# A fused retention and mixer kernel: the order of the front, VectorE's share of the query copies, and the places of two weight loads

## The chip, the cores and the metric

The kernel runs on one core of a Trainium2 chip. The metric is device time in microseconds (us). In this document TensorE, VectorE, ScalarE, GpSimd and SyncE go by the names of the profile: PE (with PEld for its weight loads), DVE, ACT, POOL and SP. SP issues the hardware DMA queue (q1 in the profile). POOL issues the software DMA queue (q0), the one that turns float32 into bf16 on its way. A tile is a buffer in on-chip memory; PSUM is the memory that PE writes and that DVE and ACT read back.

## The reference

Inputs are q, k and v of 8 batches, 8 heads, 576 positions and 64 values, in float32, and the weights of a mixer.

```python
scores = scale * np.matmul(q, k.transpose(0, 1, 3, 2))
Dmat = np.where(rel >= 0, gamma[:, None, None] ** rel[None, :, :], 0.0)
x = np.matmul(scores * Dmat, v)            # then heads side by side: (8, 576, 512)
h = x.transpose(0, 2, 1) @ U @ V           # mixing over positions, rank 32
u = x + h.transpose(0, 2, 1)
out = u + np.maximum(u @ w_ch1, 0.0) @ w_ch2   # 512 -> 2048 -> 512
```

Since the decay is a product of powers of gamma, the kernel runs attention as a recurrence over blocks of positions. It scales v by gamma to the minus position, keeps a running sum of k times v (the state), adds the masked part inside a block, and scales the result by gamma to the position.

## The kernel before

Batches go in pairs, and each pair has nine chunks of 128 positions. The first pair is treated apart, since all else waits for it. Its 1152 positions are four **units** of 256 positions (0 and 1 in batch 0, 2 and 3 in batch 1) and one chunk J, whose lower half (LO) ends batch 0 and whose upper half (HI) begins batch 1.

A unit takes these steps, with the lines of the code:

- Six loads on the SP queue, two halves each of k, q and v (`load_u`, L595), 256 KB each. Below "the second half of unit two's q" is the fourth of unit 2's six loads.
- POOL casts k and q to bf16 (`cast_u`, L613), and POOL (once DVE) scales v (`scale_u`, L617).
- PE turns k and q (`T_u`, 8 transposes at L628 each); DVE or ACT copies the turned tile out of PSUM (L639, L641). Keys (j = 1) are copied straight, queries (j = 0) are written with a step of two elements.
- PE multiplies for the scores (`SC_u`, L656), DVE masks them (`mask_u`, L664), PE multiplies by v (`RV_u`, L685), adds to the state (`ST_u`, L713; ACT copies the state in `Sblk`, L722), adds queries times state (`QS_u`, L694), and DVE writes x (`XS_u`, L702).

The half chunk J has the same steps in small (`T_J` L739, `SC_J` L752, `mask_J` L761, `RV_J` L771, `QS_J` L779, `XS_J` L786). `startup` runs units 0 and 1 and J's lower half. It then turns x (`to_xT`, L891), runs the first step of mixing (`MA`, L427: 20 matmuls into a PSUM tile that ACT casts to `a_sb`, L433), adds `a_sb` times V onto the turned x (L913), and copies the sum to `uT` (L922 on ACT, L924 on DVE). `warm` (L189) issues matmuls whose result nobody reads; they keep PE busy where it would wait.

`first_stretch` then mixes three things on PE in the order in which the code writes them: blocks of **Y1**, the first product of the channel mixer (16 blocks f0 to f15 for batch 0, four matmuls of 128x512 each, L513, each followed by a ReLU on ACT, L518), J's upper half, and units 2 and 3. Calls `y(n)` set the Y1 blocks between the others. Y1 needs the weights w1, which POOL loads in four quarters (`load_w1`, L195, 512 KB of bf16 each): quarter 0 for f0 to f3, quarter 1 for f4 to f7, and so on. POOL issues them in its program order, between its casts.

Nothing is rescheduled by a planner: the program order written here is the order on each engine, and each instruction waits for the data, the buffers and the DMAs that it needs. From about 50 us on the kernel is a steady alternation: Y1 and Y2 (L547) on PE, with attention of the following batch and DMA transposes spread between them by `merge`.

Of the kernel before, what the change touches and what calls it, by code (L numbers as in the profile page):

```python
# [9 lines left out]
FP32 = mybir.dt.float32  # L10
# [26 lines left out]
def kernel(  # L37
# [11 lines left out]
    nc = tc.nc  # L49
# [144 lines left out]
    def load_w1(fb):  # L194
        nc.gpsimd.dma_start(  # L195
            out=w1_sb[:, :, fb * W1B:(fb + 1) * W1B],
            in_=moe_w_ch1[:, fb * W1B:(fb + 1) * W1B].rearrange("(c p) f -> p c f", p=P),
        )
# [214 lines left out]
    def mixer_items(pr, par, split=False):  # L413
# [5 lines left out]

        def MA(where=None):
            pool_, tag = where or (ps_s, "pss")
            pa = pool_.tile([P, P], FP32, tag=tag, name="pa")
            for n, i in enumerate(idx):
                for cc in range(NCC):
                    nc.tensor.matmul(  # L427
                        pa[cc * R:(cc + 1) * R, :], Ub[:, n, :],
                        st["x", pr][:, i, cc * P:(cc + 1) * P],
                        start=(n == 0), stop=True, skip_group_check=True,  # L430
                    )
            a_sb = a_pool.tile([P, P], BF16, tag="a_sb", name="a_sb")
            nc.scalar.activation(out=a_sb, in_=pa, func=AF.Copy)  # L433
            st["a", par] = a_sb
            if par == 0:
                st["u", 0] = u_pool.tile([P, 4, dm], BF16, tag="u0", name="u0")
                st["uT", 0] = uT_pool.tile([P, 4, NCC, P], BF16, tag="uT0", name="uT0")
            else:
                st["u", 1] = u_pool.tile([P, 5, dm], BF16, tag="u1", name="u1")
                st["uT", 1] = uT_pool.tile([P, 5, NCC, P], BF16, tag="uT1", name="uT1")  # L440
# [54 lines left out]
        items.append(lambda: None)  # L495
        return items

    def y1_items(par, by_seg=False):
        nch = 4 + par
        segs = [(0, 4)] if par == 0 else [(0, 3), (3, 2)]  # L500
        if by_seg:
            segs = [(1, 4), (0, 1)]
        items, made = [], []

        def Y1(f, seg):
            if not made:
                made.append(1)
                st["y1", par] = y1_pool.tile(
                    [P, NF, nch * P], BF16, tag=f"y1{par}", name="y1")
            c0, n = segs[seg]  # L510
            ps = ps_big.tile([P, 4, P], FP32, tag="big", name="ps_y1")
            for cc in range(NCC):
                nc.tensor.matmul(  # L513
                    ps[:, 0:n, :], w1_sb[:, cc, f * P:(f + 1) * P],
                    st["uT", par][:, c0:c0 + n, cc, :],
                    start=(cc == 0), stop=(cc == NCC - 1),
                )
            nc.scalar.activation(  # L518
                out=st["y1", par][:, f, c0 * P:(c0 + n) * P],
                in_=ps[:, 0:n, :].rearrange("p s t -> p (s t)"), func=AF.Relu)  # L520

        ns = len(segs)
        for f in range(NF):
            items.append((nch * 216.0, lambda f=f: [Y1(f, g) for g in range(ns)]))
        if by_seg:
            return Y1, items
        return items
# [96 lines left out]
    def T_u(u, j, eng):  # L624
        pst = ps_big.tile([P, 2 * NHP, P], BF16, tag="big", name="pst")
        for jj in range(2):
            for hp in range(NHP):
                nc.tensor.transpose(  # L628
                    pst[:, jj * NHP + hp, :], un[u][j][:, jj, hp * P:(hp + 1) * P], ident)
        t = qkT_pool.tile([P, 2 * NHP, P], BF16, tag="qkT", name="qkT")  # L630
        un[u]["T", j] = t
        o, i_ = t, pst
        if j == 0:

            o = t.rearrange("p a b -> p (a b)").rearrange(
                "p (hp t j) -> p j hp t", hp=NHP, j=2)
            i_ = pst.rearrange("p (j hp) t -> p j hp t", j=2)
        if eng is nc.scalar:
            nc.scalar.activation(out=o, in_=i_, func=AF.Copy)  # L639
        else:  # L640
            eng.tensor_copy(out=o, in_=i_)  # L641

    def qT(u):
        return un[u]["T", 0].rearrange("p a b -> p (a b)").rearrange(
# [167 lines left out]
    def startup():  # L812
# [14 lines left out]
        T_u(0, 1, nc.vector)  # L827
        warm(5)
        nc.scalar.activation(out=V_b, in_=V_f, func=AF.Copy)
        T_u(0, 0, nc.scalar)  # L830
        make_v()
        warm(3)
        SC_u(0, 0, ps_sc, "psc")
# [3 lines left out]
        SC_u(0, 1, ps_o, "po")  # L837
        mask_u(0, 1)
        warm(2)
        T_u(1, 0, nc.scalar)  # L840
        scale_u(0, 0, nc.gpsimd)
        load_w1(0)
        scale_u(1, 0, nc.gpsimd)
        scale_u(1, 1, nc.gpsimd)
        cast_qk(0, J, LO, nc.gpsimd, js=(0,))
        scale_v(0, J, LO, nc.gpsimd)
        load_w1(1)
        cast_qk(0, J, HI, nc.gpsimd)
        scale_v(0, J, HI, nc.gpsimd)
        load_w1(2)  # L850
# [20 lines left out]
        warm(1, ps_big, "big")  # L871
        ST_u(1, LO, accB, False)
        Sblk(accB, 2)
        warm(1, ps_big, "big")
        RV_u(1, 0)
        RV_u(1, 1)
        T_J(LO, nc.vector)
        ST_u(1, HI, accB, False)
        Sblk(accB, 3)
        SC_J(LO)  # L880
        mask_J(LO)
        QS_u(1, 0, 1)
        QS_u(1, 1, 2)
        XS_u(1)
# [14 lines left out]
        RV_J(LO)  # L899
        QS_J(3)  # L900
        XS_J(LO)
        warm(2, ps_sc, "psc")
        xT.append(ps_sc.tile([P, dm], FP32, tag="psc", name="xT"))
        for i in range(2, J):
            to_xT(i, range(3))
        for i in range(J):
            to_xT(i, (3,))
        MA, _, _, _ = mixer_items(0, 0, split=True)
        MA((ps_o, "po"))
        warm(1)  # L910
        for cc in range(NCC):
            g = slice(cc * R, (cc + 1) * R)
            nc.tensor.matmul(  # L913
# [17 lines left out]

    def first_stretch():

        ys = iter([fn for _, fn in y1_items(0)])

        def y(n):
            for _ in range(n):
# [3 lines left out]

        _, MH0, _, outs0 = mixer_items(0, 0, split=True)
        MA1, MH1, MT1, outs1 = mixer_items(0, 1, split=True)
        y(1)
        make_uo()
        y(3)
        T_J(HI, nc.scalar, ps_s, "pss")
        y(1)
        SC_J(HI)
# [4 lines left out]
        Sblk(acc, 0)  # L954

        def unit(u, slots, last):
            if last:
                load_w1(u)
            for hh in range(2):
                cast_u(u, 1, hh, nc.gpsimd)  # L960
            cast_u(u, 0, 0, nc.gpsimd)
            cast_u(u, 0, 1, nc.gpsimd)
            if last:
                load(*order[NI], (1, 0, 2), gate=True)
                load(*order[NI + 1], (1, 0, 2))
            scale_u(u, 0, nc.gpsimd)
            scale_u(u, 1, nc.gpsimd)
            if not last:
                y(1)
            T_u(u, 1, nc.vector)  # L970
            T_u(u, 0, nc.scalar)
            y(2)
            SC_u(u, 0, ps_sc, "psc")
            mask_u(u, 0)
            y(1)
            ST_u(u, LO, acc, False)
            Sblk(acc, slots[1])
            SC_u(u, 1, ps_sc, "psc")
            mask_u(u, 1)
            if not last:  # L980
                RV_u(u, 0)
                ST_u(u, HI, acc, False)
                Sblk(acc, slots[2])
            else:
                y(1)
                load(*order[NI + 2], (1, 0, 2))
                RV_u(u, 0)
            QS_u(u, 0, slots[0])
            QS_u(u, 1, slots[1])
            RV_u(u, 1)  # L990
            XS_u(u)
            if last:
                RV_J(HI)
                XS_J(HI)
# [132 lines left out]
```

## Time and profile before

| what | us |
|---|---|
| three runs, median (lowest, highest) | 320.07 (319.88, 322.36) |
| the profiled execution, its own time | 320.66 |
| its span, first to last instruction | 318.7 |
| PE busy | 311.4 |
| DVE, ACT, POOL busy | 169.1, 136.7, 90.3 |
| PE's named waits after 50 us | 0.2 |

The span is what the trace's clock covers; 1.96 us of the execution's own time lie outside it. "Busy" adds up the durations of an engine's instructions. The profile models the ends of matmuls, so a busy PE is not necessarily at its peak. A wait is the idle time of an engine before an instruction, put down to whatever came last. The mean granted clock of PE was 1.000.

### The profile page before, as it was taken

To read this page: it belongs to the slowest core of one execution; us is meant where nothing else is said; L and a number is where in the kernel's file an instruction comes from. 1 tells how busy PE (TensorE), PEld (TensorE's weight loads), DVE (VectorE), ACT (ScalarE), POOL (GpSimd) and SP (SyncE) were. 2 spreads that over 40 slices of the span, in tenths; PEclk is the share of its full clock that TensorE was granted. 3 is DMA by queue.
4 is the path that set the end of the run, shared out by engine and by line. 5 is a ranking of instruction groups with operands and counts; after the bars stand their busy time and mean duration, and the time that the engine had idled before them with its cause. 6 is when DMAs were issued, how large, how long until landed. Compare 5 with 4: busy or idle time off the path is not lost.

```text
span 318.7 us, 9166 instructions
## 1 busy us (share of the span) xinstructions
PE 311.4 (98%) x3929; PEld 167.7 (53%) x3929; DVE 169.1 (53%) x354; ACT 136.7 (43%) x293; POOL 90.3 (28%) x138
## 2 busy tenths in 40 slices
PE   8999899999999999999999999999999999999996
PEld 3564554554444444466644444466644444467544
DVE  5571466447995467545684468545674563500012
ACT  2757557772120465038720375048720463057400
POOL 5762933512232423132241423141241300110000
DMA  7999999999999979699994999598994710620022
GB/s 202 258 204 267 232 198 203 191 203 187 237 212 216 260 156 175 137 242 183 176 184 106 262 177 175 142 248 172 163 202 109 189 37 1 135 81 0 2 84 81
DMA packets 151321, 53.30 MB, mean 167 GB/s; under 512 B 131985, under 2 KB 148753, under 8 KB 151281
## 3 DMA queue, kind: packets, MB, share of 16 engines
q1 hardware_dynamic: 144512, 40.40, 70.2%
q0 software_dynamic: 6768, 12.32, 16.2%
q8 instruction: 30, 0.49, 0.7%
q14 instruction: 11, 0.08, 0.1%
HBM read 36.85 MB, written 9.44 MB: 145 GB/s over the span
## 4 chain that ended last, share of the span: by engine, by line
PE 84%; DMA 7%; ACT 3%; DVE 2%; issue 1%; SPq 1%; POOL 1%; ACTq 0%
PE ps_y L513 37%; PE ps_y L547 35%; DMA stage_t<-in_q_dram 5%; DMA qkT<-qk 2%; PE psc L279 2%; PE ph L454 1%; PE po L344 1%; PE ps_y L558 1%; PE po L361 1%; SPq L595 1%; PE psc L290 1%; PE pa L427 1%; ACT qkT L639 1%; PE psc L656 1%; PE pst L628 1%
## 5 line engine op out<-in xcount | busy, mean ns | idle before, releaser
L518 ACT ACTIVATE y<-ps_y 128x384 bf16<-128x384 f32 (+2 forms) x192 | 89.1, 489 | 105.1 <-PE ps_y L513 104.6
L513 PE MATMUL ps_y<-uT,w_sb 128*128 128x512 bf16 (+3 forms) x768 | 132.2, 326 | 0.7 <-ACT uT L922 0.4
L547 PE MATMUL ps_y<-w_sb,y 128*128 128x512 bf16 x560 | 126.3, 379 | 0.0
L513 PEld LDWEIGHTS <-w_sb 128*128 128x128 bf16 x768 | 70.2, 98 | 51.0 <-issue 2.4
L547 PEld LDWEIGHTS <-y 128*128 128x128 bf16 x560 | 52.7, 98 | 61.3
L536 DVE TENSOR_TENSOR o_sb<-ps_y,u 128x512 f32<-128x512 f32 (+2 forms) x38 | 25.2, 663 | 66.3 <-PE ps_y L547 63.9
L303 DVE TENSOR_TENSOR ret<-psc,tri 64x256 bf16<-64x256 f32 x108 | 45.3, 419 | 1.1
L539 POOL DMA_DIRECT2D out_dram<-o_sb x31 | 17.3, 558 | 98.6 <-DVE o_sb L536 95.7
L255 POOL TENSOR_TENSOR vt<-stage_t,vscale 128x512 bf16<-128x512 f32 (+1 forms) x29 | 30.2, 1041 | 52.3 <-DMA stage_t<-in_v_dram 44.6
L325 DVE TENSOR_TENSOR s_f<-psc,s_f 128x256 f32<-128x256 f32 x42 | 17.8, 423 | 26.2 <-PE psc L290 12.9
L460 DVE TENSOR_TENSOR u<-ph,xt 128x1024 bf16<-128x1024 f32 (+3 forms) x24 | 21.8, 951 | 9.3 <-PE ph L454 9.3
L246 ACT ACTIVATE qk<-stage_t 128x512 bf16<-128x512 f32 x27 | 16.9, 626 | 21.1 <-DMA stage_t<-in_q_dram 15.2
L372 DVE TENSOR_TENSOR xt<-po,qscale 128x512 bf16<-128x512 f32 x27 | 18.4, 681 | 1.8 <-PE po L344 1.8
L244 POOL CAST qk<-stage_t 128x512 bf16<-128x512 f32 x20 | 12.3, 614 | 23.6 <-DMA stage_t<-in_k_dram 21.4
L334 ACT ACTIVATE s_sb<-s_f 128x512 bf16<-128x512 f32 (+1 forms) x27 | 15.5, 575 | 3.8 <-DVE s_f L325 3.8
L315 DVE COPY vs<-vt 64x256 bf16<-64x256 bf16 x54 | 14.3, 265 | 1.2
L664 DVE TENSOR_TENSOR ret<-psc,triU 128x1024 bf16<-128x1024 f32 x8 | 9.6, 1222 | 9.2 <-PE psc L656 9.2
L189 PE MATMUL pw<-ident 128*128 128x512 bf16 x34 | 11.5, 461 | 1.4 <-POOL ident masks.py:199 1.4
L613 POOL CAST qk<-stage_t 128x512 bf16<-128x512 f32 x16 | 9.6, 613 | 9.9 <-DMA stage_t<-in_q_dram 5.3
L323 DVE COPY s_f<-psc 128x256 f32<-128x256 f32 x6 | 2.5, 424 | 16.4 <-PE psc L290 11.3
L279 PEld LDWEIGHTS <-qkT 64*64 64x64 bf16 x432 | 5.6, 107 | 9.6 <-issue 8.5
L433 ACT ACTIVATE a_sb<-pa 128x128 bf16<-128x128 f32 x8 | 2.2, 277 | 18.0 <-PE pa L427 18.0
(112 smaller groups left out, 191.4 us busy)
## 6 DMA issues: line engine op xcount, KB each, us to landing
stage_t<-in_k_dram SPq DMA_DIRECT2D x32, 256.0 KB, 4.8
stage_t<-in_q_dram SPq DMA_DIRECT2D x32, 256.0 KB, 5.3
stage_t<-in_v_dram SPq DMA_DIRECT2D x32, 256.0 KB, 5.5
out_dram<-o_sb POOLq DMA_DIRECT2D x31, 256.0 KB, 4.3
w_sb<-in_moe_w_ch_dram POOLq DMA_DIRECT2D x4, 512.0 KB, 8.0
w_sb<-in_moe_w_ch_dram POOLq DMA_DIRECT2D x8, 256.0 KB, 5.8
stage_t<-in_k_dram SPq DMA_DIRECT2D x8, 128.0 KB, 5.1
stage_t<-in_q_dram SPq DMA_DIRECT2D x8, 128.0 KB, 5.5
```

What stands on the lines that cost most here:

```text
L246: nc.scalar.activation(out=t[rows, 0, :], in_=c["f", 0][rows].rearrange("p h d -> p (h d)"), func=AF.Copy)
L255: (eng or nc.gpsimd).tensor_tensor(out=c["v"][rows], in0=c["f", 2][rows], in1=vscale[rows, i, :, None].to_broadcast([n, H, D]), op=ALU.mult,)
L303: nc.vector.tensor_tensor(out=ret[o, n], in0=c["psc"][t, hl, 0:SW].rearrange("p (hp i) -> p hp i", i=D), in1=tri[t, None, t].to_broadcast( ...
L325: nc.vector.tensor_tensor(out=f[:, t, :], in0=inc, in1=f[:, 1 - t, :], op=ALU.add)
L334: nc.scalar.activation(out=ch[pr, i]["s1"][:, w, :], in_=s_f[:, w, :], func=AF.Copy)
L372: nc.vector.tensor_tensor(out=xt[:, i, :].rearrange("p (hp hl d) -> p hl hp d", hl=2, d=D), in0=c["po"][:, :, 0:NHP * D].rearrange("p hl ( ...
L460: nc.vector.tensor_tensor(out=st["u", par][:, i0 - base:i0 - base + n, w].rearrange("p s (c d) -> p c s d", c=2), in0=ph[k][:, :, 0:n, :], ...
L513: nc.tensor.matmul(ps[:, 0:n, :], w1_sb[:, cc, f * P:(f + 1) * P], st["uT", par][:, c0:c0 + n, cc, :], start=(cc == 0), stop=(cc == NCC - 1),)
L518: nc.scalar.activation(out=st["y1", par][:, f, c0 * P:(c0 + n) * P], in_=ps[:, 0:n, :].rearrange("p s t -> p (s t)"), func=AF.Relu)
L536: nc.vector.tensor_tensor(out=o_sb[:, 0:n], in0=ps[:, 0:n], in1=st["u", par][:, c, w], op=ALU.add)
L539: (nc.sync if last else nc.gpsimd).dma_start(out=out_flat[r0:r0 + P, w], in_=o_sb[:, 0:n])
L547: nc.tensor.matmul(ps, st["y1", par][:, f, c * P:(c + 1) * P], w2_sb[:, f, :], start=(f == 0), stop=(f == NF - 1),)
```

## The change

- In `startup` the queries of unit 0 are copied out of PSUM by DVE instead of ACT, and those of unit 1 by both: ACT the first two of four head pairs, DVE the other two.
- `T_J(LO)` moves ahead of `RV_u(1, ...)`, `SC_J` and `mask_J` move ahead of `ST_u(1, HI)`. Four of the five `warm` matmuls from there to `uT` are dropped.
- The first step of mixing of batch 0 goes in three parts (chunks 0 and 1; 2 and 3; J) between the transposes of x, into the second bank of the PSUM tile that holds the last quarter of turned x.
- The first two Y1 blocks are computed side by side: the first two of the four contraction steps of both, then the last two of both.
- `load_w1(1)` is issued ahead of the scaling of J's lower v. `load_w1(3)` is issued in unit 2, after its four casts and ahead of `scale_u(2)`, instead of at the start of unit 3.
- In unit 2 one Y1 block is placed between the transposes of the keys and those of the queries. One block fewer stands after them.

```diff
-        T_u(0, 0, nc.scalar)
+        T_u(0, 0, nc.vector)
...
-        T_u(1, 0, nc.scalar)
+        T_u(1, 0, (nc.scalar, nc.vector))
...
         cast_qk(0, J, LO, nc.gpsimd, js=(0,))
+        load_w1(1)
         scale_v(0, J, LO, nc.gpsimd)
-        load_w1(1)
...
-        warm(1, ps_big, "big")
+        T_J(LO, nc.vector)
         RV_u(1, 0)
         RV_u(1, 1)
-        T_J(LO, nc.vector)
+        SC_J(LO)
+        mask_J(LO)
         ST_u(1, HI, accB, False)
         Sblk(accB, 3)
-        SC_J(LO)
-        mask_J(LO)
...
-        warm(2, ps_sc, "psc")
-        xT.append(ps_sc.tile([P, dm], FP32, tag="psc", name="xT"))
+        MA, _, _, _ = mixer_items(0, 0, split=True)
+        last = ps_sc.tile([P, 2, dm], FP32, tag="psc", name="xT")
+        xT.append(last[:, 0, :])
+        MA(pa=last[:, 1, 0:P], ns=(0, 1))
         for i in range(2, J):
             to_xT(i, range(3))
+        MA(pa=last[:, 1, 0:P], ns=(2, 3))
+        MA(pa=last[:, 1, 0:P], ns=(4,))
         for i in range(J):
             to_xT(i, (3,))
-        MA, _, _, _ = mixer_items(0, 0, split=True)
-        MA((ps_o, "po"))
-        warm(1)
...
+        def Y1_pair():
+            st["y1", par] = y1_pool.tile(
+                [P, NF, nch * P], BF16, tag=f"y1{par}", name="y1")
+            ps = [ps_big.tile([P, 4, P], FP32, tag="big", name="ps_y1") for _ in range(2)]
+            for c2 in range(2):
+                for f in range(2):
+                    for cc in (2 * c2, 2 * c2 + 1):
+                        nc.tensor.matmul(
+                            ps[f], w1_sb[:, cc, f * P:(f + 1) * P],
+                            st["uT", par][:, 0:4, cc, :],
+                            start=(cc == 0), stop=(cc == NCC - 1),
+                        )
...
         def unit(u, slots, last):
-            if last:
-                load_w1(u)
             for hh in range(2):
                 cast_u(u, 1, hh, nc.gpsimd)
             cast_u(u, 0, 0, nc.gpsimd)
             cast_u(u, 0, 1, nc.gpsimd)
-            if last:
+            if not last:
+                load_w1(3)
+            else:
                 load(*order[NI], (1, 0, 2), gate=True)
...
             T_u(u, 1, nc.vector)
+            if not last:
+                y(1)
             T_u(u, 0, nc.scalar)
-            y(2)
+            y(2 if last else 1)
```

## The prediction

> **What bounds the kernel now.** I read the list of waits of PE first. Over the whole run it holds little:
>
> ```profile
> PE pst L628 <- POOL qk L613: 1.1, 1, 1.1
> PE ps_y L513 <- ACT uT L922: 0.4, 1, 0.4
> PE psc L656 <- ACT qkT L639: 0.3, 1, 0.3
> ```
>
> Columns: total us, times, longest. After 50 us only 0.2 us is named, so what the front gains or loses by then passes to the end almost one to one. The largest wait is unit 2's query transposes, for a POOL cast. The chain that ended last, in order of time, says what is behind that cast:
>
> ```profile
> 20.87 11.30 DMA stage_t<-in_q_dram
> 32.22 0.62 POOL qk L613
> 32.89 0.51 PE pst L628 x6
> ```
>
> A load was under way for 11.3 us. So the second question is the DMA, asked in two stretches: 28 to 30 us, then 31 to 32 us (packets, MB, share of 16 engines).
>
> ```profile
> q0 software_dynamic: 335, 0.34, 103.5%
> q1 hardware_dynamic: 148, 0.07, 16.9%
> ```
>
> ```profile
> q1 hardware_dynamic: 599, 0.30, 101.1%
> q0 software_dynamic: 27, 0.02, 13.6%
> ```
>
> While a weight quarter passes, the hardware queue moves 0.035 MB per us instead of 0.30. It all but stands. The software queue is busy like this from about 15.9 to 18.7, 21.6 to 25, 27.6 to 30.8 and 36.9 to 40.5 us: four quarters, some 3.2 us each. Their places come from POOL's order (timeline, start and duration):
>
> ```profile
> 23.58 0.80 POOL L195 DMA_DIRECT2D w_sb<-in_moe_w_ch_dram  x1
> ...
> 32.22 0.61 POOL L613 CAST qk<-stage_t 128x512 bf16<-128x512 f32 x1 [2.85 <-DMA stage_t<-in_q_dram]
> 33.20 2.07 POOL L617 TENSOR_TENSOR qk<-stage_t,vscaleU 128x512 bf16<-128x512 f32 x2 [0.37 <-DMA stage_t<-in_v_dram]
> 35.23 0.80 POOL L195 DMA_DIRECT2D w_sb<-in_moe_w_ch_dram  x1
> 36.03 2.27 POOL L613 CAST qk<-stage_t 128x512 bf16<-128x512 f32 x4
> ```
>
> POOL here waits for loads; the loads wait for earlier loads, not for compute. The front is paced by DMA from about 24 to 38 us.
>
> **The front to uT.** The relevant copies:
>
> ```profile
> 6.71 0.69 DVE L641 COPY qkT<-pst 128x1024 bf16<-128x1024 bf16 x1 [1.59 <-PE pst L628]
> 8.70 1.31 ACT L639 ACTIVATE qkT<-pst 128x1024 bf16<-128x1024 bf16 x1 [0.17 <-PE pst L628]
> 12.54 1.32 ACT L639 ACTIVATE qkT<-pst 128x1024 bf16<-128x1024 bf16 x1 [0.45 <-PE pst L628]
> 13.15 0.75 DVE L617 TENSOR_TENSOR qk<-stage_t,vscaleU 128x512 bf16<-128x512 f32 x1 [0.27 <-DMA stage_t<-in_v_dram]
> ```
>
> Unit 0's queries on DVE: no row shows DVE writing with a step of two. Bounds: 0.69 (its straight copy, above) and 1.22 (its masks of the same size, L664). ACT's stepped copy is 1.28 times its straight one (1.31 against 1.02 at 11.07), so I take 0.69 x 1.28 = 0.9, ready 0.4 earlier. Three `warm` matmuls hold PE until about 9.7, so scores start at 9.7 instead of 10.06. It ends at unit 1's last query cast (11.93), which a DMA sets.
>
> The Trainium skill ("VectorE: DVE Perf Modes", Mode 2x_1P) speaks against the edit: two results per cycle need 16-bit data at a step of one. By it the copy runs at DVE's 1x pace, an estimate of 1.2 us, and the gain is 0.1. No run here shows it yet, and the sum goes by 0.9.
>
> Unit 1's queries: in the program as built, DVE's half waits for ACT's half, although both only read PSUM. ACT's half lies between 0.54 (a 512-element ACT copy, L922) and 0.76; with 0.7 it ends at 13.25. DVE's half (0.45 to 0.65; take 0.5) ends at 13.8. Queued behind it on DVE is the scaling of unit 0's v (0.75, began 13.15), now 13.8 to 14.55, and behind that mask_u(1, 0), which began at 14.37 and now begins at 14.6. DVE's two masks and XS_u(0) (2.36 + 1.23) thus come **0.2 later**, not earlier. T_J's transposes now precede this, so DVE's T_J copy follows XS_u(0) at once: 18.6 instead of 18.78. XS_u(1) gains about 0.1 of that.
>
> Mixing in parts: from XS_u(1)'s end (21.09) to the cast of `a_sb` (22.32) took 1.23, for 10 transposes, 20 matmuls and their latency. Now 6 transposes and 8 matmuls fit in the 0.6 us until XS_J ends, then 4 matmuls follow: about 0.85, a gain of 0.4. The dropped `warm` matmuls (0.21 each) filled waits. Y1 side by side saves the 0.1 for which the first block waited on copies of `uT`. **Front: about 0.6 earlier** (bounds 0.2 and 1.0).
>
> **Unit 2 takes it back.** The Y1 blocks and J's upper half shift forward by 0.6, to the query transposes that wait for the cast at 32.89. Quarter 1 landed at 27.4, against f4's start at 27.76; issued at 17.3 instead of 19.09 it is no obstacle. One block (0.87) now stands in the wait: it was 1.11 long, becomes 1.11 + 0.6 - 0.87 = 0.8. After the transposes one block instead of two covers ACT's copy (33.44 to 34.76), so scores start at 34.82 instead of 35.06. If the q load lands as now, **0.24 is left** of 0.6 + 0.87 + the rest.
>
> **Unit 3 pays.** `load_w1(3)` is issued when POOL has cast unit 2's q, at 32.9 instead of 35.23. On POOL it pushes scale_u(2) by 0.45 (after the 0.37 idle), to end at 35.75; ST_u(2, LO) needs it at 36.0: covered. Unit 3's casts come no later. In the DMA its quarter began to flow 2.7, 2.4, 3.7 and 1.5 after the issue in the four cases; with 2.4 it starts at 35.3, not 36.9. What it meets are these (issue to landing: second halves of unit 2's k, of unit 2's q, and of unit 3's q):
>
> ```profile
> stage_t<-in_k_dram SPq DMA_DIRECT2D x1, 256.0 KB, 9.3
> ...
> stage_t<-in_q_dram SPq DMA_DIRECT2D x1, 256.0 KB, 11.3
> ...
> stage_t<-in_q_dram SPq DMA_DIRECT2D x1, 256.0 KB, 5.0
> ```
>
> The first two were in flight when a quarter began. The third, issued at 32.32, landed at 37.4 before quarter 3; now it is in the same place. Held: 3.2 us at (0.30 - 0.035)/0.30 is 2.8 us, so it lands at 40.2. Cast 0.6, and PE's transposes go on at 40.9 instead of 39.6: +1.3. The 0.2 by which f11 waited for DVE's copy of the keys goes, so **+1.1**. Bounds for the held load: 37.4 (5.0) and 43.6 (11.3); 41.6 by unit 2's k. Its allowance before PE waits is to about 38.7. Unit 3's v lands at 41 to 42 and is scaled by 43.2; ST_u(3, LO) would by then be at 44.2. Chunk loads after it shift by 2 us, but their scores come at 67.5, long after.
>
> **Sum.** 320.66 + 1.1 = 321.8 on the profiled execution. That lies 0.6 above the median of the runs shown, so against the median I forecast 320.07 + 1.1 = **321.2**. This is 0.3%; I take 1% (3.2 us) as what a measurement of this kernel can tell from no change, as the runs themselves spread by 0.8%.
>
> **The rivals.**
> 1. *The front's gain survives* (0.30). Quarter 1, earlier, may hold J's last load, hence the v scaling ahead of `load_w1(2)`, so that quarter 2 starts late and unit 2's q lands some 2.5 us earlier. Or quarter 3 starts after unit 3's q (a delay over 2.7, as one of four was). For it: loads 9.3 and 11.3 show how a little decides. Against: f8 then waits for quarter 2. Time: -0.2 (quarter 3 only late) to -1.5 (0.6 + 0.87, all kept): 318.6 to 319.9.
> 2. *Even sharing* (0.09). Beside a quarter the hardware queue keeps half, not a ninth, and unit 3's q is held 1.4: 38.8, at the allowance; net -0.2: 319.9. The 148 packets against 335 speak against it. The Trainium skill ("DMA: Bandwidth & Descriptors", Queues, rings and completion order) says that each engine takes turns between queues packet by packet, which by count would be this rival; the row at 24 to 25 us (132 against 210) agrees, that at 28 to 30 does not.
> 3. *Quarters 2 and 3 in one block* (0.11), the slower end. If J's v is held to about 25 us, quarter 2 is issued at 26 and quarter 3 behind it at 30, and both pass before nearly all of unit 3. Then its q lands at 40.5 at best, 43.6 with the 11.3 row's tail, and PE goes on at 41.2 to 44.3: +1.4 to +4.5. Over 1% it gets once that load lands after about 42.6; f8 waiting for quarter 2 beyond 35 is its sign. Middle: 323.0.
>
> Forecast 0.50. **Range** 318.9 to 322.9: it cuts the end of rival 1 and the worse half of rival 3, and takes in unit 2's k row (+2.5: 322.6). Over 1% faster would need more than all that the front has to give (0.04); over 1% slower needs the upper end of rival 3 or the 11.3 bound in the forecast's place (0.11); within 1%: 0.85.
>
> **What would show it.** Right: DVE's half copy of unit 1's queries starts after ACT's; `uT` copies start near 22.5; PE's wait at unit 2's queries stays near 0.8, with a second one of 0.7 before its scores; the software queue is busy from about 35.3; a new wait of PE at unit 3's queries of 1 us or more, ended by POOL's cast. Wrong: no wait there (rival 1 or 2), a wait of f8 on quarter 2 (3), or unit 2's q landing before 30.

## The result, and the profile after

The changed kernel took **323.15 us** (median of 18 runs, 321.17 to 326.29), the kernel before on the same chip 320.68 (18 runs, 319.88 to 323.04). The ratio is **1.0074, 95% interval 1.0048 to 1.0100**: 0.7% slower, some 2.4 us. The forecast, 321.2 with a range of 318.9 to 322.9, had the direction, and less than half of the size (1.1 us). The measured time lies 0.25 above the range. Of the 1.95 us between forecast and measurement 0.6 is the base: the kernel before took 320.07 in the runs that the forecast started from and 320.68 here. The rest, some 1.4 us, is the change. The profiled execution took 322.83 us with a span of 320.8; that of before had 320.66 and 318.7. So the two traces lie 2.1 us apart.

In the changed kernel T_u's transposes are L653 and T_J's L765, the copies L748 (ACT) and L750 (DVE and POOL), the scores L682, Y1 L534 (the pair) and L518, their ReLUs L523, the unit casts L638, the scaling of v L642, the gate of the chunk loads L224. The list of PE's waits (columns: total us, times, longest), the answer to the first view of before:

```profile
PE ps_y L518 <- ACT y L523: 1.4, 2, 1.3
...
PE pst L653 <- POOL qk L638: 1.2, 2, 0.7
PE pst L765 <- POOL qk L750: 0.6, 1, 0.6
PE pst L653 <- POOL stage_t L224: 0.4, 1, 0.4
PE ps_y L518 <- DMA w_sb<-in_moe_w_ch_dram: 0.4, 1, 0.4
PE xT L916 <- ACT a_sb L438: 0.4, 1, 0.4
```

The wait of 1.1 at unit 2's queries is gone. In its place stand three others: waits at unit 3's queries (0.55 and 0.45, the second put down to POOL's next instruction), 0.43 for weight quarter 2 in unit 2, and a new one of 1.26 that ends on ACT. (The rest of these rows lies in the front: 0.70 at 8.1 us, in the row of the unit casts, 0.61 at J's transposes and 0.38 at the transposes of x.) The timeline of PE shows the first two at unit 3 (start, duration, in brackets the idle time ahead):

```profile
38.70 0.62 PE L653 MATMUL pst<-ident,qk 128*128 128x128 bf16 x8
39.87 0.28 PE L653 MATMUL pst<-ident,qk 128*128 128x128 bf16 x2 [0.55 <-POOL qk L638]
40.61 0.51 PE L653 MATMUL pst<-ident,qk 128*128 128x128 bf16 x6 [0.45 <-POOL stage_t L224]
```

In the kernel before these were 16 transposes without a pause:

```profile
39.06 1.07 PE L628 MATMUL pst<-ident,qk 128*128 128x128 bf16 x16
```

The block behind them starts at 40.95 instead of 39.96. POOL's timeline shows why, and what else became late:

```profile
30.34 0.74 POOL L195 DMA_DIRECT2D w_sb<-in_moe_w_ch_dram  x1
...
36.03 0.61 POOL L638 CAST qk<-stage_t 128x512 bf16<-128x512 f32 x1 [0.43 <-DMA stage_t<-in_k_dram]
39.20 1.35 POOL L638 CAST qk<-stage_t 128x512 bf16<-128x512 f32 x2 [2.56 <-DMA stage_t<-in_q_dram]
40.49 0.16 POOL L224 MEMSET stage_t<- 1x1 f32 x3
```

Quarter 3 is issued at 30.34 instead of 35.23. From 33.6 to 36.7 it holds the hardware queue; DMA between 34 and 36 us (packets, MB, share of 16 engines):

```profile
q0 software_dynamic: 323, 0.33, 99.0%
q1 hardware_dynamic: 187, 0.09, 18.5%
```

Unit 3's q then lands at 39.2. The two casts behind it end at 40.5, and behind *them* on POOL stand the three small memsets that gate the loads of the following chunks. In the kernel before they ran 2.2 us earlier:

```profile
38.25 0.16 POOL L224 MEMSET stage_t<- 1x1 f32 x3
```

So the first chunk's loads leave 2.2 us later. What comes of that is in the chain that ended last (start, duration):

```profile
43.52 12.54 DMA stage_t<-in_q_dram
...
56.08 0.63 ACT qk L246
56.71 0.49 ACT y L523
...
57.24 1.89 PE ps_y L518 x8
```

The same in the timelines of ACT and PE:

```profile
56.08 0.63 ACT L246 ACTIVATE qk<-stage_t 128x512 bf16<-128x512 f32 x1 [1.85 <-DMA stage_t<-in_q_dram]
```

```profile
57.24 1.89 PE L518 MATMUL ps_y<-uT,w_sb 128*128 128x512 bf16 x8 [1.26 <-ACT y L523]
```

The q load of the second chunk lands 12.5 us after its issue, at 56.06. ACT has the cast of this q in its order, and the ReLUs of Y1 behind it. PE needs a ReLU to free its PSUM buffer, and waits 1.26. In the kernel before this cast waited for nothing:

```profile
53.35 0.62 ACT L246 ACTIVATE qk<-stage_t 128x512 bf16<-128x512 f32 x1
```

The gate is only the beginning of that delay. In the kernel before the load of this q was issued at 43.85, no earlier than here, and landed 8.4 us later. What passes beside it is different: the loads of the second weights, w2 (`load_w2`, L201), which POOL issues behind the same casts. Before, three of them were issued from 40.40 on and passed from about 42 to 47 us, and the hardware queue was free behind them. Here they are issued from 42.89 on and pass from about 46 to 51, and a fourth, issued at 47.70 instead of 51.26, follows from 52 to 54. While they pass, the hardware queue moves little, with this q in it (48 to 49 us):

```profile
q0 software_dynamic: 190, 0.19, 111.7%
q1 hardware_dynamic: 58, 0.01, 8.6%
```

The account of the 2.1 us between the two traces, as the place of the changed kernel against that of before at the same work: first copy of `uT` 0.36 late (23.44 against 23.08); unit 2's scores 0.36 early (34.70 against 35.06); unit 3's block 0.99 late; its scores 0.78 late; behind the ACT wait, at the sixth group of chunk scores, 2.02 late (93.44 against 91.42).

### The profile page after: what moved, and what is told of

Its sections match the earlier page's. It is cut to its first block, busy times and chain, and to the rows that moved or that the text cites. A ratio compares the mean times of both kernels' runs of the same rounds, so it can differ in the third digit from the quotient of the medians.

```text
span 320.8 us, 9157 instructions
## 1 busy us (share of the span) xinstructions
PE 310.5 (97%) x3925; PEld 167.1 (52%) x3925; DVE 170.4 (53%) x356; ACT 134.7 (42%) x292; POOL 90.7 (28%) x138
## 3 DMA queue, kind: packets, MB, share of 16 engines
q1 hardware_dynamic: 144512, 40.40, 67.5%
q0 software_dynamic: 6768, 12.32, 15.5%
## 4 chain that ended last, share of the span: by engine, by line
PE 80%; DMA 11%; SPq 5%; ACT 2%; POOL 1%; issue 1%; DVE 0%; POOLq 0%; ACTq 0%
PE ps_y L572 39%; PE ps_y L518 33%; DMA stage_t<-in_q_dram 6%; DMA stage_t<-in_v_dram 3%; SPq L620 3%; PE psc L279 2%; DMA stage_t<-in_k_dram 2%; SPq L230 1%; PE po L344 1%; PE ps_y L583 1%; PE po L361 1%; PE ph L459 1%; PE psc L290 1%; PE pa L430 1%; ACT y L523 1%
## 5 line engine op out<-in xcount | busy, mean ns | idle before, releaser
L518 PE MATMUL ps_y<-uT,w_sb 128*128 128x512 bf16 (+3 forms) x760 | 130.5, 326 | 2.0 <-ACT y L523 1.4
L523 ACT ACTIVATE y<-ps_y 128x512 bf16<-128x512 f32 (+3 forms) x190 | 87.9, 488 | 104.8 <-PE ps_y L518 104.1
L518 PEld LDWEIGHTS <-w_sb 128*128 128x128 bf16 x760 | 69.4, 98 | 51.1 <-issue 2.8
L244 POOL CAST qk<-stage_t 128x512 bf16<-128x512 f32 x20 | 12.3, 613 | 25.6 <-DMA stage_t<-in_k_dram 17.7
L334 ACT ACTIVATE s_sb<-s_f 128x512 bf16<-128x512 f32 (+1 forms) x27 | 15.5, 576 | 9.1 <-DVE s_f L325 7.4
L638 POOL CAST qk<-stage_t 128x512 bf16<-128x512 f32 x16 | 9.8, 613 | 8.7 <-DMA stage_t<-in_q_dram 5.2
L189 PE MATMUL pw<-ident 128*128 128x512 bf16 x30 | 9.9, 462 | 1.4 <-POOL ident masks.py:199 1.4
```

What stands on the lines that cost most here:

```text
L334: nc.scalar.activation(out=ch[pr, i]["s1"][:, w, :], in_=s_f[:, w, :], func=AF.Copy)
L518: nc.tensor.matmul(ps[:, 0:n, :], w1_sb[:, cc, f * P:(f + 1) * P], st["uT", par][:, c0:c0 + n, cc, :], start=(cc == 0), stop=(cc == NCC - 1),)
L523: nc.scalar.activation(out=st["y1", par][:, f, c0 * P:(c0 + n) * P], in_=ps[:, 0:n, :].rearrange("p s t -> p (s t)"), func=AF.Relu)
```

## The experiments

Each ratio is against the kernel before, run in turn with it on one chip, with its 95% interval; different experiments ran on different chips, so they are compared by their ratios. Where an expectation names its theories by letters, W is that quarter 3's new place makes the loss (W2: by way of late chunk loads), F that the front makes it. Each trace is one execution, and executions differ by 1 to 3 us, so medians carry the verdicts and traces the mechanisms. The kernels stand here by what they tell.

**Quarter 3 back, the rest of the change kept.**

```diff
             if not last:
-                load_w1(3)
...
         def unit(u, slots, last):
+            if last:
+                load_w1(u)
```

> The changed kernel with the third weight quarter issued at the start of unit 3 again, all else as changed. Theory W (the quarter passes ahead of unit 3's loads, so PE waits at unit 3's queries, and the chunk loads, which are gated behind POOL's casts, come late enough to block ACT): both waits go, about 1.1 and 1.3 us; the gain up to unit 2's scores (34.70 instead of 35.06) stays. Time about 0.4 below the kernel before, 320.3. Rival F (the front's own edits are what costs, uT copies start at 23.44 instead of 23.08): the time stays within 0.5 of the changed kernel, 322.7 to 323.2.

It took 320.87 us, a ratio of **0.9988 [0.9959, 1.0018]**. There is no wait at unit 3's queries, and its transposes are one run:

```profile
38.11 1.07 PE L653 MATMUL pst<-ident,qk 128*128 128x128 bf16 x16
```

PE waits for ACT near 57 no more. The whole loss goes with one line, and what is left of the change can't be told from nothing. F falls.

**Quarter 3 alone**, in the kernel before: the opposite edit, and nothing else of the change.

> The kernel before with nothing but the third weight quarter moved: issued in unit 2, after its four casts and ahead of scale_u(2). Theory W: the same two waits appear, at unit 3's queries and in ACT ahead of the PE wait near 57 us. Unit 2's queries still come at 32.2, so the quarter starts later than in the changed kernel: +1 to +2.4, 321.7 to 323.1. Rival (the quarter hurts only when the second weight quarter is late as well, since both then pass in one block): within 0.5 of the kernel before.

It took 321.75 us, **1.0044 [1.0011, 1.0077]**. The waits at unit 3's queries are there (0.40 and 0.47), and the late chunk loads show further on, at the sixth group of chunk scores, which needs a DMA transpose:

```profile
93.47 0.32 PE L279 MATMUL psc<-qkT 64*64 64x64 bf16 x16 [0.83 <-DMA qkT<-qk]
```

**Quarter 1 at its old place**, the rest of the change kept.

```diff
+        scale_v(0, J, LO, nc.gpsimd)
         load_w1(1)
-        scale_v(0, J, LO, nc.gpsimd)
```

> The changed kernel with the second weight quarter (the one for Y1 blocks 4 to 7) issued behind the scaling of J's lower v again. Theory W: J's upper loads are no longer held, the third of the four quarters goes out near 23.6 instead of 25.3, unit 2's queries land at 32 instead of 29.7 again and PE waits there about 0.8; the last quarter then still passes ahead of part of unit 3. Time 321.5 to 323. Rival: the early second quarter is itself what costs; then the time falls to the kernel before's 320.7 or below.

It took 322.32 us, 1.0054 [1.0022, 1.0086]. Unit 2's q still landed early (its last cast at 28.84, where 32 was expected), and unit 3's waits stayed (0.38 and 0.45). In this trace neither needs quarter 1's new place.

**ACT's late cast out of the way**: the cast of the second chunk's q and its DMA transpose are written behind six more Y1 blocks.

```diff
-        prep(NI + 1)
+        cast_qk(*order[NI + 1], eng=nc.vector, js=(1,))
+        scale_v(*order[NI + 1])
...
                 gated_w2(2 * f, f - 1)
+        cast_qk(*order[NI + 1], eng=nc.scalar, js=(0,))
+        xbar(*order[NI + 1])
         MH1((5, 6, 7, 8))
```

> The changed kernel with ACT's cast of the queries of the second chunk of batch 2 (the one that ACT waits for at 56.08, PE then waiting 1.26) and that chunk's DMA transpose placed behind six Y1 blocks more; its keys' cast and its v stay. If the in-order ACT is what carries the late chunk load to PE, the 1.26 goes and nothing takes its place, since its scores come at about 74: 321.9. Rival (the late DMA transpose or the chunk loads behind it on the SP queue make PE wait later instead): no gain, 322.8 to 323.5.

It took 322.88 us, 1.0052 [1.0019, 1.0085], which can't be told from the changed kernel. The wait for ACT at 57 is gone, but a wait of 0.96 for a DMA transpose stands at 93.14. So ACT's cast is only one of the places where the lateness reaches PE; taking that place away moves the wait. In this trace PE had already waited 1.25 for quarter 2 in unit 2, and so came to unit 3's queries late enough to find them cast.

**Half of quarter 3 early, half at unit 3.**

```diff
             if not last:
-                load_w1(3)
+                load_w1h(3, 0)
...
+            if last:
+                load_w1h(3, 1)
```

> The changed kernel with the last weight quarter loaded in two halves: the half for Y1 blocks 12 and 13 in unit 2, where the change put the quarter, the half for blocks 14 and 15 at the start of unit 3, where the kernel before had it. Theory W (the quarter holds the hardware queue while it passes, some 3 us for 512 KB): half of it passes ahead of unit 3, its loads are held half as long, and about half of the loss goes: 321.5 to 322 against 320.2 before. Rival (what counts is the place on POOL's queue, not the bytes): as the whole quarter, +0.4 to +0.9%.

It took 321.19 us, **1.0008 [0.9976, 1.0040]**, less than the 321.5 to 322 that were expected. There is no wait at unit 3's queries, and the gate ran at 39.07 instead of 40.49. Its trace still has a wait of 1.0 us for ACT near 56, for the same q cast, whose load took 12.3 us here too. So it is no cure for the second cost in every execution; the median shows little of it.

**Quarter 3 right behind quarter 2**, earlier still.

```diff
         load_w1(2)
+        load_w1(3)
...
             if not last:
-                load_w1(3)
```

> The changed kernel with the last weight quarter issued directly behind the third one in the startup, ahead of unit 2's casts too. Theory W: the two quarters pass in one block of some 6 us, unit 2's queries land about 3 us later (33 to 35 instead of 29 to 30) and PE waits there 2 to 3 us more; unit 3's loads and the chunk loads are held no more than in the changed kernel. Time 323 to 325. Rival (an earlier quarter only fills idle DMA time): as the changed kernel or below, 322.5.

It took 322.49 us, 1.0048 [1.0019, 1.0077]; expected were 323 to 325, a miss. Not unit 2's q was held but its v (scaled at 34.36 after 3.69 of waiting, which cost PE nothing). PE still waited at unit 3's queries (0.27 and 0.46).

This trace and that of the kernel with quarter 1 back are each the fastest of twelve runs (320.62 and 320.56). In both the gate ran late, at 39.6 to 39.7, and yet neither ACT's cast near 53 us nor PE near 57 or 91 waited for a chunk load. So late chunk loads don't cost something in every execution, and what the slower runs of these two kernels lost is in no trace.

**Late chunk loads alone.** The kernel with quarter 3 back, and the gate some 2 us later, behind POOL's scaling of unit 3's v.

```diff
-                load(*order[NI], (1, 0, 2), gate=True)
-                load(*order[NI + 1], (1, 0, 2))
             scale_u(u, 0, nc.gpsimd)
             scale_u(u, 1, nc.gpsimd)
+            if last:
+                load(*order[NI], (1, 0, 2), gate=True)
+                load(*order[NI + 1], (1, 0, 2))
```

> The changed kernel with the last quarter at its old place (so that unit 3's loads are not held), but the first two chunk loads of batch 2 issued 2 us later, behind scale_u(3) instead of ahead of it. Theory W2 (late chunk loads alone reach PE, through ACT's query cast ahead of the ReLUs near 57 us, or through a DMA transpose later): +1 against the kernel with the quarter at its old place, 321 to 321.9. Rival (the chunk loads have 2 us to spare, and only unit 3's own loads matter): no difference, 319.8 to 320.8.

It took 321.50 us, **1.0041 [1.0009, 1.0072]**, against 0.9988 in the earlier comparison without this edit. The gate ran at 39.76 instead of 37.28, the loads of w2 hardly later (39.86 instead of 39.64), and PE waited for nothing at unit 3's queries. The lateness of the chunk loads alone costs about 0.5%, and shows at the same group of scores:

```profile
91.18 0.32 PE L279 MATMUL psc<-qkT 64*64 64x64 bf16 x16 [0.87 <-DMA qkT<-qk]
```

**Early chunk loads, quarter 3 as changed.** The other half of the separation: the gate ahead of the casts of unit 3's q.

```diff
             for hh in range(2):
                 cast_u(u, 1, hh, nc.gpsimd)
+            if last:
+                load(*order[NI], (1, 0, 2), gate=True)
+                load(*order[NI + 1], (1, 0, 2))
             cast_u(u, 0, 0, nc.gpsimd)
             cast_u(u, 0, 1, nc.gpsimd)
```

> The changed kernel, with the six gated chunk loads issued ahead of the casts of unit 3's q instead of behind them (some 4 us earlier, at about 36.5). It tells the two parts of the loss apart. Theory: the late chunk loads cost about 1.1 us and the hold of unit 3's q about 0.8 to 1.0, so the first part goes, the second stays: waits of 0.7 to 1.2 in sum at unit 3's queries, no wait of PE over 0.4 at 57 or at 93, ratio 1.002 to 1.005 against the kernel before, 321.0 to 321.9. Rival, the late loads cost nothing by themselves: ratio as the changed kernel's, 1.006 to 1.009. Rival, the hold costs nothing: 0.998 to 1.001.

It took 321.15 us, **1.0018 [0.9992, 1.0044]**. POOL's timeline, then ACT's:

```profile
35.58 0.16 POOL L224 MEMSET stage_t<- 1x1 f32 x3
38.34 1.35 POOL L638 CAST qk<-stage_t 128x512 bf16<-128x512 f32 x2 [2.61 <-DMA stage_t<-in_q_dram]
```

```profile
53.27 0.62 ACT L246 ACTIVATE qk<-stage_t 128x512 bf16<-128x512 f32 x1
```

Unit 3's q is held here too, though PE loses only 0.38 by it in this trace; the gate no longer stands behind it, and the cast on ACT waits for nothing. The load of its q was issued at 41.52 and landed after 5.3 us, ahead of most of the loads of w2. These were issued late all the same (42.07), so their lateness alone is not what costs. Of the 0.74% some 0.2% stay, for the hold by itself, and the interval reaches to zero. The rest, 0.5 to 0.6%, is put down to the chunk loads, in agreement with the run before this one; that the edit shortened the hold a little as well is not excluded.

**Both kernels again**, for a second trace each.

> The kernel before, unchanged, for a second trace. Theory: its 1.1 us wait at unit 2's queries (a q load that landed at 32.2) is not in every execution, since in every later trace of any kernel that load landed by 30.3, also where the front was that of before. Then no wait over 0.5 us stands there, and the stretch from the first Y1 block to f10 is 15.5 to 15.7 us in place of 16.23. If the wait belongs to the kernel, it is there again with 0.9 to 1.3 us and the stretch is near 16.2.

> The changed kernel, unchanged, for a second trace. Theory: the hold of unit 3's q (1.0 us of waits at its queries) and the late cast of the second chunk's q (a wait of PE of 1 us near 57) belong to the kernel: first Y1 block to f10 16.4 to 17.0, f10 to 57 near 17.7 to 18.1, unless the second wait shows at the DMA transpose near 91 to 93 instead (0.8 to 1.0). Rival, that both were accidents of one execution: neither wait over 0.4 us.

Each is one run. The kernel before took 321.69 here. Unit 2's last q cast ran at 29.70, in place of 32.22, and nothing waited at its queries. From the first Y1 block to unit 3's block it took 14.97 us, less than expected (15.5 to 15.7). In 19 of the 20 traces of this study that cast starts before 30; the profile of before, on which the prediction was worked out, is the one that differs. The changed kernel took 321.64, in the lower part of its runs. Its second trace has the hold at unit 3 (0.47 and less), 0.80 for quarter 2 in unit 2, and near 57 nothing; the late chunk loads appear at the transpose instead:

```profile
92.24 0.32 PE L279 MATMUL psc<-qkT 64*64 64x64 bf16 x16 [0.64 <-DMA qkT<-qk]
```

**The parts of the front.** First: mixing in parts, with the last transposes ahead of its last part; the Y1 pair; the block between unit 2's transposes; all else as before.

```diff
-        MA(pa=last[:, 1, 0:P], ns=(4,))
         for i in range(J):
             to_xT(i, (3,))
+        MA(pa=last[:, 1, 0:P], ns=(4,))
```

> Of the change only three parts: mixing's first step in parts, with the last four transposes of x put ahead of its last part (they share a PSUM tile with it and waited for the cast to a_sb), Y1's first two blocks side by side, and one Y1 block between unit 2's transposes. Queries on ACT, J's order, and both weight quarters as in the kernel before. uT copies at about 22.7 instead of 23.08 (before) and 23.44 (changed); scores of unit 2 0.4 to 0.9 earlier; no wait at unit 3. If the front passes to the end one to one: 0.4 to 0.9 below the kernel before, 319.4 to 319.9. Rival (waits for DMA take it back): within 0.2 of it.

It took 320.20 us, 0.9987 [0.9965, 1.0009], no gain that can be measured.

Then the front with unit 2's blocks in their old order (and quarter 3 back):

```diff
             T_u(u, 1, nc.vector)
-            if not last:
-                y(1)
             T_u(u, 0, nc.scalar)
-            y(2 if last else 1)
+            y(2)
```

> The changed kernel with quarter 3 at the start of unit 3 and with the older order of the blocks in unit 2 (both groups of transposes in a row, two blocks behind them); the front, Y1 side by side and quarter 1's place stay changed. Theory: where unit 2's q lands at 28 to 30, the two blocks cover the copy of the queries, which one block leaves open by 0.58, so this runs 0.5 us below the kernel with only quarter 3 put back (0.9988): 0.996 to 0.998, 319.1 to 319.8; from the first Y1 block to unit 2's scores about 10.0 us in place of 10.61. Rival, the order of the blocks doesn't matter to the end: 0.9985 to 1.0005. Rival, the front has lost time and the blocks don't matter: over 1.001.

It took 321.02 us, 1.0013 [0.9984, 1.0043], above what was expected, though the trace shows the mechanism that was: from the first Y1 block to unit 2's scores 9.99 us instead of 10.61. Lines of this kernel:

```profile
33.74 0.42 PE L682 MATMUL psc<-qkT 64*64 64x128 bf16 x16
...
91.67 0.32 PE L279 MATMUL psc<-qkT 64*64 64x64 bf16 x16 [1.68 <-DMA qkT<-qk]
```

PE reached unit 3's block at 38.65, 1.3 ahead of the profile of before, and gave 1.7 back at 91, where it had come too early for the transpose.

The order of the blocks alone, in the kernel before:

> The kernel before, with only unit 2's blocks in the changed order (one between the transposes of the keys and of the queries, one behind them). Theory: +0.5 us, ratio 1.0008 to 1.0025, 320.6 to 321.2, with a wait of 0.5 to 0.6 before unit 2's scores for ScalarE's copy and no wait at its queries. Rival (the forecast's step): unit 2's q is late, the block between fills that wait, -0.2 to -0.9 us: 0.997 to 0.9995.

It took 320.93 us, 1.0010 [0.9984, 1.0035]; the median lies where the theory put it, the interval takes in both. The trace has 10.68 us from the first Y1 block to unit 2's scores, against 10.07 in the second trace of before: the 0.6 us, in the stretch if not in the verdict.

The front without DVE's copies of the queries (as the front alone, with ACT copying both):

> As the kernel with the front alone changed, but with the queries of units 0 and 1 copied by ScalarE as before. The stepped copy took VectorE 1.30 us against ScalarE's 1.31, so theory: no difference of more than 0.3 us to the front alone, ratio 0.995 to 0.999, first Y1 block within 0.4 us of it. Forecast's step (VectorE 0.9): 0.2 to 0.4 us slower than the front alone.

It took 320.28 us, 0.9998 [0.9971, 1.0026]. The first Y1 block starts at 23.56, against 23.75 with the copies on DVE. They bring nothing that can be measured.

**Tries for a kernel that beats both**, with the early chunk loads: the changed kernel with quarter 3 back; the front alone; the front alone without DVE's copies; the kernel before.

> The changed kernel with quarter 3 back at the start of unit 3, and the chunk loads issued ahead of the casts of unit 3's q. A try for a kernel that beats both. Theory: where the chunk loads are in time, earlier ones bring nothing: ratio 0.997 to 1.000, 319.4 to 320.4, as with quarter 3 back alone (0.9988). If the chunk loads were still late in the kernel before (its first DMA transpose landed just in time), up to 1 us more: 0.994 to 0.996.

> The front alone changed (quarter 3 and the order of unit 2's blocks as before), with the gated chunk loads ahead of the casts of unit 3's q. Theory: the chunks' transposes move ahead by 1 to 2 us, the wait near 91 goes or falls under 0.5, and the front's gain reaches the end: 0.995 to 0.998, 318.8 to 319.7. Rival, the transpose near 91 is not set by these loads: the wait of 1 to 2 us stays, 0.999 to 1.002.

> The same, with ScalarE copying the queries of units 0 and 1 as before. Theory: within 0.3 us of the run with the front and early chunk loads, 0.995 to 0.998. Rival as there: 0.999 to 1.002.

> The kernel before, with only the chunk loads ahead of the casts of unit 3's q. Theory: no named wait after 50 us over 0.3 us was there to win, except in executions where the transpose near 91 is late: 0.998 to 1.0005. Rival, that transpose holds the kernel before in many of its executions: 0.994 to 0.997.

In this order they took 320.47 us, 0.9997 [0.9972, 1.0022]; 320.52, 1.0006 [0.9983, 1.0029]; 320.65, 1.0008 [0.9980, 1.0036]; 320.22, 1.0005 [0.9979, 1.0031]. None beats the kernel before, and the gain expected of the second and third (0.995 to 0.998) did not come. Early chunk loads bring nothing where they weren't late, and the front's gain doesn't reach the end even with them: the second of the four still waits 0.75 at 90.87. The third, which shows no such wait, has the shortest span of all (317.2 us, 319.13 in its own time), yet the median of its runs isn't lower. Why is open.

The stages of nine traces, starts in us:

| kernel | first Y1 block | unit 2's scores | unit 3's block | sixth chunk scores | span |
|---|---|---|---|---|---|
| before | 23.73 | 35.06 | 39.96 | 91.42 | 318.7 |
| before, again | 26.18 | 36.25 | 41.15 | 92.44 | 319.8 |
| changed | 24.09 | 34.70 | 40.95 | 93.44 | 320.8 |
| changed, again | 23.56 | 34.50 | 40.29 | 92.24 | 319.6 |
| quarter 3 back | 23.50 | 34.11 | 39.01 | 90.46 | 317.9 |
| late chunk loads | 23.44 | 34.06 | 38.96 | 91.18 | 318.9 |
| early chunk loads | 24.20 | 34.81 | 40.09 | 91.17 | 318.7 |
| front alone | 23.75 | 33.74 | 38.65 | 91.67 | 319.7 |
| front alone, no DVE copies, early loads | 23.14 | 33.13 | 38.03 | 89.37 | 317.2 |

From unit 2's scores to unit 3's block it takes 4.90 or 4.91 in all but the two traces of the changed kernel (6.25, 5.79) and the one with early chunk loads (5.28): that is the hold. From the sixth group of chunk scores to the end it takes 227.3 to 228.0 in all nine: from there on the kernels differ by some 0.7 at most.

## Why the prediction was wrong

**"Chunk loads after it shift by 2 us, but their scores come at 67.5, long after."** This is the step that failed. The shift was right (gate 2.24 us later); its price was put at nothing, by the first consumer of the chunk in PE's program. But between the load and those scores stand three things: the loads of w2, which in the changed kernel pass while the second chunk's q is under way; ACT's cast of the second chunk's q with the ReLUs of Y1 behind it; and SP's queue with the DMA transposes. The runs give the price: 0.5% (1.7 us) when only these loads are late (1.0041 against 0.9988), and 0.56% won back when only they are early (1.0018 against 1.0074). Each of these ratios is uncertain by some 0.3%, so each difference by some 0.4%. By these medians it was the larger part of the loss. How much of it goes by each of the three ways is open. The look for named waits after 50 us in the profile of before showed that PE had lost next to nothing there, not how near the next wait was. The transpose for the sixth group of chunk scores landed at 91.37 and PE used it at 91.42; the weight load for these scores had already waited for it:

```profile
91.42 0.21 PEld L279 LDWEIGHTS <-qkT 64*64 64x64 bf16 x16 [0.60 <-DMA qkT<-qk]
```

The group came 4.36 us after the fifth, against 4.19 where the chunk loads are early. There was no slack left. So what the front gains does not pass to the end one to one either, as the prediction had it: the front alone came 1.3 early to unit 3's block and waited 1.7 at this group.

**"Unit 3 pays"** was right in its mechanism and nearly in its numbers. Quarter 3 began to flow at 33.6 (forecast 35.3), it held unit 3's q to 39.2 (forecast 40.2), and PE's block came at 40.95, +1.0 on before; the forecast said +1.1. Its issue came earlier than forecast, since unit 2's q wasn't late. In the medians the hold is worth less: 0.2% (0.6 us, with an interval that reaches down to nothing) with the chunk loads out of the way. That the forecast's 1.1 of hold came near to half of the measured loss is thus partly luck.

**The front "about 0.6 earlier"** is not to be seen in the first trace, which is 0.36 later. Over the traces it is within its bounds: the first Y1 block starts at 23.53 in the median of 14 traces with T_J moved ahead (23.14 to 24.20), at 23.91 in the five whose front is that of before (23.73 to 26.18). The one trace left, with only parts of the front, has 24.29. The two groups overlap, so 0.4 earlier is likely, not shown. Most of its parts were wrong:

- Unit 0's queries on DVE were taken at 0.9. Timelines of DVE and ACT in the changed kernel:

```profile
8.66 1.30 DVE L750 COPY qkT<-pst 128x1024 bf16<-128x1024 bf16 x1 [1.73 <-PE pst L653]
...
13.19 0.73 DVE L750 COPY qkT<-pst 128x512 bf16<-128x512 bf16 x1 [0.35 <-ACT qkT L748]
```

  1.30 us, not 0.9, above both ends of the bounds (0.69 and 1.22); ACT took 1.31. The straight copy is 0.69 on the same engine: the step of two costs DVE nearly a factor of two, ACT a factor of 1.28 (1.31 against 1.02), and the guess carried ACT's factor over to DVE. Here the Trainium skill's rule ("VectorE: DVE Perf Modes", Mode 2x_1P), that two results per cycle need 16-bit data at a step of one, agrees with the row. The estimate of 1.2 by that rule was nearer than the 0.9 that the sum used.
- DVE's half of unit 1's queries did start behind ACT's, and took 0.73, where 0.5 was taken. The masks behind it came at 14.40 instead of 14.37, so the 0.2 of delay was not there.
- J's transposes, moved ahead, waited 0.61 in the first trace for POOL's cast of J's q, whose load was late (cast at 17.20, before at 16.66). The prediction had no such wait. In the second trace there was none, and the first Y1 block came at 23.56 instead of 24.09.
- Mixing in parts was to gain 0.4, from XS_J's end to the first copy of `uT`. It took 1.40 before and 1.41 after. The last transposes of x write the PSUM tile that also holds the mixing's sum, and four of them wait 0.38 for ACT's read of that sum (`a_sb`). With the transposes ahead of the last part it took 1.51.

**"Unit 2 takes it back"** came true by another cause. Its q landed at 29.7, so there was neither the forecast wait of 0.8 at its queries nor a late q to blame it on. What takes the gain up to unit 2's scores is the step that the prediction itself counted second: one block behind the transposes doesn't cover ACT's copy of the queries. It leaves 0.56 to 0.58 open in five traces, or the time goes to the wait for quarter 2 (0.43 and 0.80 in the two of the changed kernel). Two blocks behind the transposes cover it, 9.99 us from the first Y1 block against 10.61, where quarter 2 is in time; in the trace with ACT copying both, PE waited 0.81 for that quarter. Front and unit 2 together come to 0.9988 [0.9959, 1.0018], as the forecast's sum of next to nothing for them had it: the right number by luck.

**The rivals.** That the front's gain survives has both its signs in the traces, unit 2's q before 30 and f8 waiting for quarter 2, and still not its time: unit 3 and the chunk loads took more than the front gave. Nor was the cause of the early q the rival's, since it came early also with quarter 1 back and in the second trace of before. Even sharing of the queues would have meant no wait at unit 3; beside quarter 3 the hardware queue got 187 packets against 323, and q was held. The Trainium skill's turn-taking packet by packet ("DMA: Bandwidth & Descriptors", Queues, rings and completion order) shows in part of that count: it was 138 against 149 from 34 to 35 us, 49 against 174 from 35 to 36. With quarter 3 right behind quarter 2 it was 142 against 143 from 31 to 32 us, and even so the hardware queue moved 0.07 MB in that time, not 0.30. What decides whether the turns are even is open; either way the hardware queue is held. Quarters 2 and 3 in one block did not happen by itself, and when it was made to happen (quarter 3 right behind quarter 2) it cost no more than the other places, 1.0048; that is 1.5 us, at the lower end of its price of 1.4 to 4.5.

**The base.** The prediction took 1.11 us of waiting in unit 2 from one execution as a fact of the kernel. A second trace had none. The size of the miss hardly rests on it, but the whole working of that part did.

## What to carry to other kernels

When a load or an issue moves, follow every instruction that stands behind it in each engine's order, small ones too: here three memsets of 0.16 us in all, behind a late cast, were by the medians worth more than the late cast. Follow what the moved issue will then meet in the queues as well. "Used long after" is measured at the first in-order engine or queue that has to touch the data (a cast, a transpose, a queue's slot), and how much slack that one has can be read from the trace, as the distance between its landing and its use. And look at two executions before a single wait becomes the base of a sum.

## What was not expected of the hardware

- The second trace of before has a pause of 1.05 us of PE, with nothing in the profile that it waited for, and a stretch at half the clock behind it. PE in the middle of 32 alike matmuls, and the windows behind (us, busy of each engine, granted clock, DMA share, GB/s):

```profile
17.24 0.34 PE L685 MATMUL po<-qk,ret 64*128 64x64 bf16 x11
18.64 0.49 PE L685 MATMUL po<-qk,ret 64*128 64x64 bf16 x21 [1.05 <-issue]
```

```profile
19.00:20.00 1.00, 0.85 (x41) 0.69 (x33) 0.42 (x1) 0.25 (x1) 1.00 (x2) 1.00 1.37 174
20.00:21.00 1.00, 1.00 (x21) 0.96 (x18) 0.72 (x2) 0.82 (x3) 0.62 (x1) 0.77 1.31 161
21.00:22.00 1.00, 1.00 (x13) 0.74 (x12) 1.00 (x1) 0.23 (x1) 0.00 (x0) 0.50 1.11 165
22.00:23.00 1.00, 1.00 (x6) 0.55 (x7) 0.52 (x2) 0.00 (x0) 0.34 (x1) 0.50 1.19 182
23.00:24.00 1.00, 1.00 (x9) 0.72 (x8) 0.26 (x1) 0.00 (x0) 0.88 (x2) 0.53 1.24 205
24.00:25.00 1.00, 1.00 (x27) 0.54 (x24) 0.00 (x0) 0.22 (x1) 0.94 (x1) 1.00 1.20 227
```

  The granted clock is 0.50 for some 3.4 us, from about 20.5 to 23.9, and the first Y1 block comes 2.45 us later than in the first trace. The Trainium skill ("TensorE: Matmul & The Clock Gate", Part 1) tells of a gate that grants half the clock after an idle window of about 3.4 us and the full clock after a busy one. The half clock and its length agree. PE was not idle for a window, though: it was busy for 2.30 of the 3.5 us from 17.0 to 20.5. Five other traces have a pause of 0.33 to 0.55 us among these same matmuls, and their clock stayed at 1.00. What stopped PE is not shown, and that the pause brought the half clock is argued from the order of the two.
- Which of several loads a passing weight quarter holds changes with a shift of a microsecond or two: unit 2's q in one trace of before, its v in most others, unit 3's q where quarter 3 comes earlier. What the quarters cost can't be read from one of them.
